# Splitting each of a weight's four loads into two transfers of rows

## The chip, the cores and the metric

The kernel runs on one core of a Trainium2 chip. The metric is the device time of one execution in microseconds (us). A measurement gives the median of several executions; three of the kernel before gave 159.38, 159.83 and 160.25 us.

## The reference

Two layers follow one another. The first is a linear attention with a decaying state: for each of 4 batches and 8 heads, 768 steps with heads 48 wide. The second mixes along the sequence through two low-rank matrices U and V (rank 32) and then along the channels through two weights, `w_ch1` (384 x 1536) and `w_ch2` (1536 x 384), with a ReLU between them.

```python
for t in range(S):
    state = alpha[:, :, t, :, None] * state + np.einsum('bhd,bhe->bhde', k[:, :, t], v[:, :, t])
    y[:, :, t] = np.einsum('bhd,bhde->bhe', q[:, :, t], state)
...
xt = x.transpose(0, 2, 1)
h = xt @ U @ V
u = x + h.transpose(0, 2, 1)
ch = np.maximum(u @ w_ch1, 0.0) @ w_ch2
return (u + ch).astype(np.float32)
```

## The kernel before

The sequence of 768 steps is cut into 6 chunks of 128. For each batch the kernel works through the chunks: it loads alpha, k, q and v of a chunk (four transfers of 192 KB), takes logarithms of alpha and sums them along the chunk with a matmul, scales k and q with the exponentials, and forms scores, state and output with matmuls. In some chunks two groups of heads are worked on as a pair. Then come the low-rank mix (`stage_mix`) and the two products with the weights: `mlp1` with `w_ch1` (L788 in the profile) and `mlp2` with `w_ch2` (L816).

Every piece of work is an operation of a plan (class `Plan`). Its order over all engines is a table of characters written out by hand or by a tool: three characters for each operation, which name it and the engine that does it. Each engine runs its own operations strictly in that order. A DMA is an operation too; nearly all are issued by SP (SyncE), in the table's order. Their completions are told by eight semaphores used in turn, so that an issue also waits until the transfer eight issues before it has landed.

The weights come from memory as float32 and are kept in SBUF as bfloat16. `weights` does this for both. `weights1` calls it for `w_ch1` with four groups of 384 columns (groups 0 to 3, operations `wload1 0` to `wload1 3`). One load (L323) brings a group as 128 partitions x 3 x 384 elements of 4 bytes, 576 KB, into the buffer `ws`, which lies in the memory of the second `h1t` tile (`h1t` in the profile). Three casts (L280 on ScalarE, L284 on GpSimd) then turn its three slices into bfloat16 in `w_sb`. The table issues the groups in the order 3, 1, 0, 2. `weights2` loads `w_ch2` in three transfers of 768 KB into the same buffer, once the casts have read it.

`mlp1` of the first batch needs a group for each three of its twelve slices `jt`: slice `jt` uses group `jt // 3`. In TensorE's order the first three products with the weight use group 3, and the fifth (with three matmuls each) is the first that uses group 1, the twelfth the first that uses group 0. Group 2 is used later, after other work.

Of the kernel before, what the change touches and what calls it, by code (L numbers as in the profile page):

```python
# [153 lines left out]
def kernel(  # L154
# [29 lines left out]
    def slots(name, n, shape, dtype):  # L184
        return [const.tile(shape, dtype, name=f"{name}{i}") for i in range(n)]

    PAIRS = {0: 3, 1: 3, 2: 0, 3: 0}
    QUEUE_T = tuple((3, c) for c in range(6))
    LAST, CUT = 3, 240
# [2 lines left out]
    P = Plan()  # L192
# [85 lines left out]
    def copy(eng, dst, src):  # L278
        if eng == "ACT":
            nc.scalar.copy(dst, src)  # L280
        elif eng == "DVE":
            nc.vector.tensor_copy(dst, src)  # L282
        else:
            nc.gpsimd.tensor_copy(dst, src)  # L284

    def queue(eng):
        return nc.scalar if eng == "ACT" else nc.sync
# [26 lines left out]
    ws = h1_s[1].bitcast(FP32)  # L314
# [5 lines left out]
    def weights(name, n, src, dst):  # L320
        for g in range(len(dst) // n):
            keys = [("ws", g * n + i) for i in range(n)]
            P.add(f"{name} {g}", lambda e, g=g: queue(e).dma_start(ws[:, g * n : (g + 1) * n, :], src(g)), w=keys)  # L323
            for i in range(n):
                to, key = dst[g * n + i]
                op = P.add("wcast", lambda e, to=to, x=g * n + i: copy(e, to, ws[:, x, :]), r=[keys[i]], w=[key])
                casts.setdefault(g * n + i, []).append(op)

    def weights1():
        cs = [slice(g * DM, (g + 1) * DM) for g in range(4)]  # L330
        weights(
            "wload1", NCT, lambda g: moe_w_ch1[:, cs[g]].rearrange("(c p) n -> p c n", p=128),
            [(w1_sb[:, ct, cs[g]], ("w1", g, ct)) for g in range(4) for ct in range(NCT)],
        )

    def weights2():
        weights(
            "wload2", 4, lambda g: moe_w_ch2[g * 512 : (g + 1) * 512, :].rearrange("(j p) n -> p j n", p=128),
            [(w2_sb[:, jt, :], ("w2", jt)) for jt in range(NJ)],
        )  # L340
# [3 lines left out]
    def paired(b, c):  # L344
        return c // 2 < PAIRS[b]

# [535 lines left out]
```

## Time and profile before

| what | us |
|---|---|
| median of three executions | 159.83 |
| lowest and highest | 159.38, 160.25 |
| the profiled execution's own time | 159.11 |
| its span in the profile | 157.3 |

The profile shows one execution. The span runs from the first to the last instruction of the program; the rest of the execution's time lies around it. PE is TensorE's matmul, PEld its weight load, DVE VectorE, ACT ScalarE, POOL GpSimd and SP SyncE. SPq stands for SP's queue of issues: the duration of such a row is how long SP was busy with an issue or held by it, not how long the data moved. The page's table of slices cuts the span in 40 equal parts; its row for TensorE reads

```profile
PE   6869899999989999999999999999999999999992
```

where each digit is the busy share in tenths (9 is 90% or more). Its DMA issues for the first weight (four transfers) and the second (three) are these, with the median time from issue to landing last:

```profile
h1t<-in_moe_w_ch_dram SPq DMA_DIRECT2D x4, 576.0 KB, 6.6
h1t<-in_moe_w_ch_dram SPq DMA_DIRECT2D x3, 768.0 KB, 8.7
```

### The profile page before, as it was taken

The numbers are of one execution on the slowest core, as the hardware profiler recorded it, in microseconds if no ns is written. First come the engines' busy times: TensorE is split into PE (matmuls) and PEld (weight loads), VectorE is DVE, ScalarE is ACT, GpSimd is POOL, SyncE is SP. The second block draws the span as 40 slices with busy tenths as digits, with TensorE's granted clock in tenths as the row PEclk, the third lists the DMA queues.
The fourth block names the chain that finished last, engine by engine and source line by source line (L and its number), as shares of the span: only waits on it lengthen the run. The fifth ranks groups of instructions, "written<-read, shape, count | busy, mean of one in ns | idle before, by whom it ended". The sixth has DMA issues, their size and how long they took to land.

```text
span 157.3 us, 4541 instructions
## 1 busy us (share of the span) xinstructions
PE 150.0 (95%) x1769; PEld 98.4 (63%) x1769; DVE 113.6 (72%) x252; ACT 85.0 (54%) x222; POOL 58.7 (37%) x94
## 2 busy tenths in 40 slices
PE   6869899999989999999999999999999999999992
PEld 2457676866767566766667656666657556665571
DVE  6349988996999348586999968698889247854151
ACT  3768887978867764749798484263612101061000
POOL 8188676465797110350726462048500000000000
PEclk9999999999999999999999999999999999999999
DMA  5999999997999799999999984899950556572425
GB/s 129 305 307 292 262 262 279 362 301 192 320 324 338 166 197 208 212 217 181 200 221 197 206 161 88 169 197 189 203 124 4 150 99 102 155 214 79 155 76 183
DMA packets 94230, 31.57 MB, mean 201 GB/s; under 512 B 87904, under 2 KB 94176, under 8 KB 94208
## 3 DMA queue, kind: packets, MB, share of 16 engines
q1 hardware_dynamic: 93680, 31.07, 81.9%
q8 instruction: 14, 0.23, 0.5%
q10 hardware_dynamic: 528, 0.20, 0.5%
q14 instruction: 8, 0.07, 0.1%
HBM read 23.79 MB, written 4.72 MB: 181 GB/s over the span
## 4 chain that ended last, share of the span: by engine, by line
PE 86%; SPq 3%; DMA 2%; POOL 2%; DVE 2%; issue 1%; ACT 1%; POOLq 0%; DVEq 0%; ACTq 0%
PE ps L816 30%; PE ps L788 29%; PE ps L431 3%; PE ps L737 3%; DMA io<-in_alpha_dram 2%; SPq L353 2%; PE ps L624 2%; PE ps L538 2%; PE ps L596 2%; PE ps L489 2%; POOL rkq L414 2%; PE ps L455 2%; PE ps L691 2%; PE ps L562 1%; PE ps L757 1%
## 5 line engine op out<-in xcount | busy, mean ns | idle before, releaser
L788 PE MATMUL ps<-uT,w_sb 128*128 128x384 bf16 x288 | 51.6, 326 | 0.5 <-DVE sm L518 0.5
L816 PE MATMUL ps<-w_sb,h1t 128*128 128x384 bf16 (+2 forms) x300 | 51.9, 320 | 0.0
L798 ACT ACTIVATE h1t<-ps 128x384 bf16<-128x384 f32 x49 | 23.1, 498 | 29.4 <-PE ps L788 29.4
L816 PEld LDWEIGHTS <-h1t 128*128 128x128 bf16 x300 | 27.5, 98 | 16.5 <-issue 0.6
L788 PEld LDWEIGHTS <-w_sb 128*128 128x128 bf16 x288 | 26.7, 98 | 16.6 <-issue 0.8
L800 DVE TENSOR_SCALAR h1t<-ps 128x384 bf16<-128x384 f32 x47 | 24.5, 550 | 5.3 <-PE ps L788 5.0
L822 DVE TENSOR_TENSOR io<-ub,ps 128x384 f32<-128x384 bf16 (+2 forms) x25 | 12.8, 533 | 13.9 <-PE ps L816 13.9
L738 DVE TENSOR_TENSOR ub<-xb,ps 128x384 bf16<-128x384 bf16 x24 | 12.1, 550 | 6.9 <-PE ps L737 6.6
L466 DVE TENSOR_TENSOR pm<-ps,maskp 128x512 bf16<-128x512 f32 x24 | 15.7, 681 | 0.5 <-PE ps L455 0.4
L634 DVE TENSOR_TENSOR pm<-ps,maskc 128x512 bf16<-128x512 f32 x24 | 15.3, 682 | 0.8 <-PE ps L624 0.8
L583 POOL TENSOR_TENSOR rkq<-io,aa 128x384 bf16<-128x384 f32 x8 | 7.3, 915 | 18.9 <-ACT aa L573 8.9
L583 POOL TENSOR_TENSOR rkq<-io,ai 128x384 bf16<-128x384 f32 x10 | 9.1, 914 | 10.1 <-PE ps L596 3.9
L414 POOL TENSOR_TENSOR rkq<-io,aa 128x384 bf16<-128x384 f32 x11 | 10.1, 923 | 7.2 <-DMA io<-in_q_dram 5.8
L280 ACT CAST xb<-ps 128x192 bf16<-128x192 f32 (+1 forms) x23 | 7.6, 360 | 8.5 <-PE ps L691 6.7
L280 ACT COPY kqt<-ps 128x512 bf16<-128x512 bf16 x15 | 8.9, 590 | 3.5 <-PE ps L431 1.8
L431 PE MATMUL ps<-ident,rkq 128*128 128x128 bf16 x96 | 8.4, 220 | 1.6 <-POOL rkq L414 1.6
L282 DVE COPY kqt<-ps 128x512 bf16<-128x512 bf16 x21 | 8.3, 416 | 2.3 <-PE ps L431 1.5
L414 POOL TENSOR_TENSOR rkq<-io,ai 128x384 bf16<-128x384 f32 x10 | 9.0, 912 | 1.1 <-PE ps L489 0.5
L573 ACT ACTIVATE aa<-ps 128x384 bf16<-128x384 f32 x12 | 6.0, 502 | 4.9 <-PE ps L564 4.1
L431 PEld LDWEIGHTS <-rkq 128*128 128x128 bf16 x96 | 6.0, 97 | 3.2 <-POOL rkq L414 2.3
L383 ACT ACTIVATE lt<-io 128x384 bf16<-128x384 f32 x12 | 6.2, 528 | 3.0 <-DMA io<-in_alpha_dram 2.9
L284 POOL CAST rv<-io 128x384 bf16<-128x384 f32 x14 | 7.0, 506 | 2.1 <-DMA io<-in_v_dram 1.6
(113 smaller groups left out, 220.8 us busy)
## 6 DMA issues: line engine op xcount, KB each, us to landing
io<-in_k_dram SPq DMA_DIRECT2D x24, 192.0 KB, 3.9
io<-in_q_dram SPq DMA_DIRECT2D x24, 192.0 KB, 3.9
io<-in_v_dram SPq DMA_DIRECT2D x24, 192.0 KB, 4.1
io<-in_alpha_dram SPq DMA_DIRECT2D x23, 192.0 KB, 4.0
h1t<-in_moe_w_ch_dram SPq DMA_DIRECT2D x4, 576.0 KB, 6.6
h1t<-in_moe_w_ch_dram SPq DMA_DIRECT2D x3, 768.0 KB, 8.7
out_dram<-io SPq DMA_DIRECT2D x24, 96.0 KB, 2.2
out_dram<-io SPq DMA_DIRECT2D x11, 192.0 KB, 1.9
```

Source lines behind the costliest of these rows:

```text
L280: nc.scalar.copy(dst, src)
L414: eng.tensor_tensor(jh(dst()[:, :, 0:D]), raw(a), jh(x()), op=ALU.mult)
L431: nc.tensor.matmul(dst, lhsT=ring()[:, HP * j + 2 * a : HP * j + 2 * a + 2, :].rearrange("t h w -> t (h w)"), rhs=ident, start=True, stop= ...
L466: nc.vector.tensor_tensor(dst, s2, maskp.to_broadcast([C, 2, 2, C]), op=ALU.mult)
L583: eng.tensor_tensor(dst()[:, :, 0:D], a(), x(), op=ALU.mult)
L634: nc.vector.tensor_tensor(pm()[:, :, par, :], s2, maskc.to_broadcast([C, HP, C]), op=ALU.mult)
L738: P.add(f"u {b}.{c}", lambda e, c=c, hb=hb: nc.vector.tensor_tensor(ub()[:, c, :], xb()[:, c, :], hb()[:, 0:DM], op=ALU.add), r=[hb] + xk( ...
L788: nc.tensor.matmul(hb()[:, 0:TW], lhsT=w1_sb[:, ct, jt * 128 : (jt + 1) * 128], rhs=u_half(uT, ct, tt, b in QUEUE_U), start=(ct == 0), sto ...
L798: nc.scalar.activation(dst, hb()[:, 0:TW], AF.Relu)
L800: nc.vector.tensor_scalar_max(dst, hb()[:, 0:TW], 0.0)
L816: nc.tensor.matmul(hb()[:, 0 : hi - lo], lhsT=h1()[:, jt, c * C : (c + 1) * C], rhs=w2_sb[:, jt, lo:hi], start=(jt == 0 and b not in INPLA ...
L822: P.add(f"out_{hi - lo} {b}.{c}", lambda e, hb=hb, lo=lo, hi=hi: nc.vector.tensor_tensor(flat(ou)[:, lo:hi], (xb if b in INPLACE else ub)( ...
```

## The change

A small table `ROWS` names, for each group of the first weight, how many of the 128 rows (partitions) the first transfer brings. A second transfer brings the rest. Both land in the same buffer and belong to the same operation of the plan, and the casts read the buffer after both. The second weight isn't in the table; its loads remain whole.

```diff
+    ROWS = {("wload1", 3): 120, ("wload1", 1): 104, ("wload1", 0): 120, ("wload1", 2): 88}
...
-            P.add(f"{name} {g}", lambda e, g=g: queue(e).dma_start(ws[:, g * n : (g + 1) * n, :], src(g)), w=keys)
+
+            def f(e, g=g):
+                cut = ROWS.get((name, g), 128)
+                for rows in (slice(0, cut), slice(cut, 128)):
+                    if rows.start < 128:
+                        queue(e).dma_start(ws[rows, g * n : (g + 1) * n, :], src(g)[rows])
+
+            P.add(f"{name} {g}", f, w=keys)
```

On SP, where the first three loads of the weight (groups 3, 1 and 0) are issued, the order before is this; `h1t_73` is the buffer of the weight, `io_...` are the buffers of k, q, v and alpha, and x2 stands for two such issues in a row.

```order
L353 DMA io_167<-in_q_dram 128x4x96
L323 DMA h1t_73<-in_moe_w_ch_dram 128x3x384 x2
L353 DMA io_168<-in_k_dram 128x4x96
L323 DMA h1t_73<-in_moe_w_ch_dram 128x3x384
L353 DMA io_169<-in_alpha_dram 128x4x96
L353 DMA io_170<-in_q_dram 128x4x96
```

With the change it is this; L331 is the line of the weight's loads now, and L363 that of the others.

```order
L363 DMA io_167<-in_q_dram 128x4x96
L331 DMA h1t_73<-in_moe_w_ch_dram 120x3x384
L331 DMA h1t_73<-in_moe_w_ch_dram 8x3x384
L331 DMA h1t_73<-in_moe_w_ch_dram 104x3x384
L331 DMA h1t_73<-in_moe_w_ch_dram 24x3x384
L363 DMA io_168<-in_k_dram 128x4x96
L331 DMA h1t_73<-in_moe_w_ch_dram 120x3x384
L331 DMA h1t_73<-in_moe_w_ch_dram 8x3x384
L363 DMA io_169<-in_alpha_dram 128x4x96
L363 DMA io_170<-in_q_dram 128x4x96
```

Three issues are added here; the loads of k, alpha and q keep their places among the rest and stand two, three and three issues further back.

Where the fourth load (group 2) is issued on SP, the order before is

```order
L353 DMA io_173<-in_v_dram 128x4x96
L353 DMA io_134<-in_k_dram 128x4x96
L323 DMA h1t_73<-in_moe_w_ch_dram 128x3x384
L353 DMA io_135<-in_v_dram 128x4x96
L353 DMA io_136<-in_k_dram 128x4x96
```

and with the change

```order
L363 DMA io_173<-in_v_dram 128x4x96
L363 DMA io_134<-in_k_dram 128x4x96
L331 DMA h1t_73<-in_moe_w_ch_dram 88x3x384
L331 DMA h1t_73<-in_moe_w_ch_dram 40x3x384
L363 DMA io_135<-in_v_dram 128x4x96
L363 DMA io_136<-in_k_dram 128x4x96
```

The loads of v and k behind it stand four issues further back. Nothing moves on the other engines: their instructions and their order are the same.

## The prediction

> **What bounds the kernel now.** I read the page's table of engines first, then stages cut where the change begins, then TensorE's own waits.
>
> ```profile
> PE 150.0 (95%) x1769; PEld 98.4 (63%) x1769; DVE 113.6 (72%) x252; ACT 85.0 (54%) x222; POOL 58.7 (37%) x94
> 0.00:24.00 24.00, 20.16 (x352) 13.66 (x353) 16.44 (x54) 17.06 (x44) 16.44 (x34) 1.00 0.98 259
> 24.00:44.00 20.00, 20.00 (x302) 13.84 (x302) 18.16 (x42) 16.66 (x43) 12.05 (x20) 1.00 1.01 292
> 44.00:50.00 6.00, 5.47 (x149) 4.16 (x142) 5.70 (x13) 4.48 (x15) 4.94 (x9) 1.00 1.03 329
> 50.00:155.00 105.00, 104.36 (x986) 66.79 (x983) 73.35 (x145) 46.84 (x122) 25.25 (x35) 1.00 0.76 165
> ```
>
> The stage rows give, after the stretch and its length, the busy time of PE, PEld, DVE, ACT and POOL, the granted clock (1.00 everywhere), the DMA share and GB/s. Up to 24 us TensorE loses 24.00 - 20.16 = 3.84 us; the DMA share there is 0.98, so this first stage waits for data. From 24 to 155 us it is busy 20.00 + 5.47 + 104.36 = 129.83 of 131.00 us. Behind 24 us the kernel is bound by TensorE with 1.17 us lost: 0.53 between 44 and 50 us and 0.64 after that.
>
> ```profile
> 23.88 1.62 SPq L323 DMA_DIRECT2D h1t<-in_moe_w_ch_dram  x2
> 25.54 1.48 SPq L353 DMA_DIRECT2D io<-in_k_dram  x1
> 27.07 0.74 SPq L323 DMA_DIRECT2D h1t<-in_moe_w_ch_dram  x1
> 27.86 0.49 SPq L353 DMA_DIRECT2D io<-in_alpha_dram  x1
> 28.39 1.43 SPq L353 DMA_DIRECT2D io<-in_q_dram  x1
> 29.86 1.75 SPq L353 DMA_DIRECT2D io<-in_v_dram  x1
> 31.66 0.68 SPq L353 DMA_DIRECT2D io<-in_q_dram  x1
> 32.38 1.45 SPq L353 DMA_DIRECT2D io<-in_v_dram  x1
> 33.94 1.84 SPq L353 DMA_DIRECT2D io<-in_k_dram  x1
> 35.83 0.66 SPq L323 DMA_DIRECT2D h1t<-in_moe_w_ch_dram  x1
> 36.58 0.43 SPq L353 DMA_DIRECT2D io<-in_v_dram  x1
> ```
>
> These are SP's rows of the timeline (start, duration, what). The four loads of the first weight are issued at 23.88 (parts 3 and 1, one behind the other), 27.07 (part 0) and 35.83 (part 2). So nothing before 23.88 us can change, and what the change can win is at most the 1.17 us that TensorE loses behind it: 0.7% of this execution's 159.11 us (span 157.3 and 1.81 around it). What it can cost has no such lid.
>
> **The change part by part.** *More issues.* Four transfers are added on SP. A plain issue takes 0.43 to 0.68 us there (27.86, 31.66, 36.58), take 0.51, so 2.04 us of SP's time. Three of them come before 33.94 us, where five issues last 1.48, 1.43, 1.75, 1.45 and 1.84 us. Against 0.51 each that is 7.95 - 2.55 = 5.40 us in which SP was held, and I read this as transfers queued faster than they drain. Three more issues, 1.53 us, are taken out of that 5.40 and cost nothing. If the queue had room there, they would push the four loads behind them by 1.53 us. The fourth stands behind 35.83 and is not covered: v at 36.58 and the three loads behind it go 0.51 us later. Their readers:
>
> ```profile
> 37.04 1.78 POOL L414 TENSOR_TENSOR rkq<-io,aa 128x384 bf16<-128x384 f32 x2 [2.04 <-DMA io<-in_q_dram]
> 39.04 0.91 POOL L414 TENSOR_TENSOR rkq<-io,ai 128x384 bf16<-128x384 f32 x1 [0.22 <-PE ps L788]
> 42.94 1.78 POOL L414 TENSOR_TENSOR rkq<-io,ai 128x384 bf16<-128x384 f32 x2
> 44.68 2.04 POOL L414 TENSOR_TENSOR rkq<-io,aa 128x384 bf16<-128x384 f32 x2
> io<-in_k_dram SPq DMA_DIRECT2D x2, 192.0 KB, 4.9
> ```
>
> At 4.9 us to landing, the k issued at 37.11 to 38.27 is there at 42.0 to 43.2 us; the two products at 42.94 each take 0.89, so the second begins at 43.83: 0.6 us to spare against 0.51. I take zero.
>
> *The data.* The bytes are the same, 576 KB a load. What is not in the trace is how the rows of a transfer of 120, 104 or 88 rows are laid over the 16 DMA engines, since every load before has 128 (v_in 32). I bound the landing from two sides.
>
> ```profile
> 28.00:30.00 2.00, 2.00 (x38) 1.65 (x36) 2.00 (x5) 1.94 (x8) 1.20 (x2) 1.00 1.05 364
> 35.40:36.40 1.00, 1.00 (x9) 0.59 (x6) 1.00 (x3) 1.00 (x4) 0.00 (x0) 1.00 0.24 58
> GB/s 330 437 227 146 146 192 165 158 165 211 284 303 277 238 173 108 65 54 50 46 19 19 23 19 84 169 157 119 146 219 296 315 277 242 181 161 123 223 96 65
> ```
>
> While weights flow, 364 GB/s: one load takes 589,824 B / 364 = 1.62 us, and one engine of 16 carries 364 / 16 = 22.8 GB/s. *Upper end:* each small part runs behind its big one as long as its rows ask for, on engines that are already full: 1.62 us x 8/120, 24/104, 8/120, 40/88 = 0.11, 0.37, 0.11, 0.74. *Lower end,* below nothing: in the last row (40 slices of 0.1 us from 34 us on) the rate falls to 19 GB/s from 36.0 to 36.4 us, less than one engine's. So one engine was still at work long after the rest: from 35.4 to 36.4 us the moved rate is 58 GB/s, and the issue at 33.94 is held until 35.78. If the split spares this late engine its rows, each load could land earlier by up to the second that the tail shows, 1.0 us. Between -1.0 and the sums (0.11, 0.48, 0.59 for the three that follow one another; 0.74 for part 2, in front of which the queue ran empty), I take zero: the same engines and rate as the nearest row, the 128-row load.
>
> *What a landing is worth to TensorE.* The casts and the first product of the weight:
>
> ```profile
> 30.29 0.50 POOL L284 CAST w_sb<-h1t 128x384 bf16<-128x384 f32 x1 [1.02 <-DMA h1t<-in_moe_w_ch_dram]
> 30.49 0.97 ACT L280 CAST w_sb<-h1t 128x384 bf16<-128x384 f32 x2
> 31.85 0.96 POOL L284 CAST w_sb<-h1t 128x384 bf16<-128x384 f32 x2 [1.06 <-DMA h1t<-in_moe_w_ch_dram]
> 34.04 0.96 POOL L284 CAST w_sb<-h1t 128x384 bf16<-128x384 f32 x2 [0.76 <-DMA h1t<-in_moe_w_ch_dram]
> 40.89 0.93 ACT L280 CAST w_sb<-h1t 128x384 bf16<-128x384 f32 x2 [0.27 <-DMA h1t<-in_moe_w_ch_dram]
> 31.69 6.01 PE L788 MATMUL ps<-uT,w_sb 128*128 128x384 bf16 x36
> 42.39 1.14 PE L788 MATMUL ps<-uT,w_sb 128*128 128x384 bf16 x6
> ```
>
> The idle time in brackets says that these casts begin as the load lands: 30.29, 31.85, 34.04, 40.89. Part 3: ScalarE's casts end at 31.46, TensorE starts at 31.69, and 0.20 us lie between landing and the casts' start, so 0.43 us are free. Part 1 is wanted by the fifth of the twelve groups of three: 31.69 + 12 x 0.162 = 33.63 (36 matmuls until 37.53), POOL is done at 32.81: 0.82 free. Part 0 is wanted by the twelfth, 31.69 + 33 x 0.162 = 37.04, done at 35.00 on POOL: 2.0 free. Part 2 is wanted at 42.39, ScalarE is done at 41.82: 0.57 free. The upper end uses 0.11 of 0.43, 0.48 of 0.82, 0.59 of 2.0, and 0.74 of 0.57: only part 2 reaches TensorE, by 0.17 us. An earlier landing wins nothing at these four places, because TensorE has no gap there (20.00 of 20.00 us): it is late for its own earlier work, not for the weight.
>
> *The 0.53 us.*
>
> ```profile
> 46.25 0.65 PE L788 MATMUL ps<-uT,w_sb 128*128 128x384 bf16 x3 [0.53 <-DVE sm L518]
> ```
>
> This wait ends with a VectorE sum, not with a load. It can go or stay with the way that POOL's work falls beside VectorE's; bounds -0.53 and 0, I take half, -0.26.
>
> **Sum:** 159.11 + 0 (issues) + 0 (landings) - 0.26 = 158.85 for the profiled execution. That execution lies 0.72 below the median of the runs shown, 159.83; carried to the median: **159.6 us**.
>
> [...] The trace does not show which engines carry which rows. [...]
>
> **The rivals.** *A, faster: the late engine is spared.* For it: the 19 GB/s tail, the 1.84 us issue behind it, and POOL's 2.04 us of waiting for q at 37.04. The loads behind part 0 would land up to 1.0 us earlier and SP would go on earlier. Against it: TensorE has only 1.17 us to give back, of which no part ends with a load. If all 0.53 goes, and the runs' 0.72 over the profile is also time lost to late loads, 159.83 - 1.25 = **158.6**.
>
> *B, slower: the late engine gets more.* The mechanism is the landing of part 2. If its rows fall on engines that carry the big part too, and the late engine is one of them, the four extra lots add up, 0.11 + 0.37 + 0.11 + 0.74 = 1.33 us, against 0.57 free: TensorE waits 0.76 us at 42.39 us. The casts of part 2 must also be over before the second weight's loads overwrite the buffer:
>
> ```profile
> 42.04 1.04 SPq L323 DMA_DIRECT2D h1t<-in_moe_w_ch_dram  x2
> 49.24 0.95 ACT L280 CAST w_sb<-h1t 128x384 bf16<-128x384 f32 x2
> 50.63 0.82 PE L816 MATMUL ps<-w_sb,h1t 128*128 128x384 bf16 x4
> ```
>
> There the second weight is cast until 50.19 and wanted at 50.63, so 0.44 is free for the first of them; the one behind it goes out later by the same 0.76. I price a second wait of equal size for it: 159.83 + 1.52 = **161.3**. The point from which B decides: part 2 landing more than 0.57 us later. For it: of the three later loads the one landing at 40.89 has the least room, and its small part, 40 rows, is the largest. Against it: the queue had run empty in front of it (0.24 share), so lags need not add up.
>
> *C: it does not do what it says.* The rows stay spread evenly over all engines, whatever their number; then four issues are all that remains, and the time is that of the forecast without the half of 0.53: 159.8.
>
> **How the numbers follow.** Forecast 0.36, C 0.12, A 0.28, B 0.24. The likeliest time is 159.6, and its own range 159.1 to 160.5. The range over the cases reaches to A's 158.6, and to B's 161.3: **158.6 to 161.3**; what lies outside is A with more than 1.25 us or B with a third wait. A measurement of this kernel can tell about 0.5% from no change, 0.8 us. A's 158.6 is 0.77% below the median, B's 0.9% above it, so the chances are 0.28 faster, 0.48 the same, 0.24 slower.
>
> **What the changed profile would show.** Forecast right: TensorE again loses about 1.2 us between 24 and 155 us, and its first product of the weight starts within 0.1 us of 31.69. A: SP's held issues shrink (1.84 at 33.94 first), POOL's 2.04 us wait for q goes, the tail of 19 GB/s near 36 us is gone, and casts begin before 30.29, 31.85 and 34.04. B: ScalarE's casts of part 2 begin after 41.5 us and TensorE shows a gap before the product that stood at 42.39, and another near 50 to 53 us. The issue term is wrong if the loads behind 36.58 land more than 0.6 us later and POOL waits for k at 43.8. The forecast as a whole is wrong if time changes before 23.88 us, where nothing was touched.

## The result, and the profile after

The changed kernel takes 165.72 us (median of three executions, 165.42 to 166.05) against 159.83 us (159.38 to 160.25). The ratio is 1.037 with a 95% interval of 1.0315 to 1.0425: slower by 5.89 us, far outside the range of the prediction. The profiled execution took 166.05 us, its span is 164.3 us, 7.0 more than before. The times and ratios of the experiments below leave out executions that took over 1.5% longer than the fastest of the same kernel (two of four of e4, one of four of e5, two of ten of e1, e9 and e12, one of ten of e11), and the profiles of e1, e4 and e9 show such executions.

From the page of the kernel after: busy time of each engine, granted clock in 40 slices, DMA packets, and the costliest group.

```profile
PE 152.4 (93%) x1768; PEld 99.1 (60%) x1769; DVE 114.0 (69%) x252; ACT 84.9 (52%) x222; POOL 59.1 (36%) x94
PEclk9999999999986999999999999999999999999999
DMA packets 94258, 31.57 MB, mean 192 GB/s; under 512 B 87932, under 2 KB 94204, under 8 KB 94236
L798 PE MATMUL ps<-uT,w_sb 128*128 128x384 bf16 x288 | 53.6, 330 | 4.4 <-POOL w_sb L287 4.0
```

L798 is the product that was L788, L331 the weight's loads, L283 and L287 the casts on ScalarE and GpSimd. The last row is new in kind: TensorE stood idle for 4.4 us ahead of this product, 4.0 of it for weights that GpSimd had not cast yet. The same stretches as in the prediction, after the change:

```profile
0.00:24.00 24.00, 19.83 (x351) 13.68 (x353) 16.31 (x54) 16.87 (x44) 15.61 (x33) 1.00 0.99 258
24.00:44.00 20.00, 17.43 (x228) 11.00 (x230) 15.25 (x34) 14.21 (x36) 9.80 (x15) 1.00 1.00 224
44.00:50.00 6.00, 4.02 (x48) 2.37 (x47) 3.45 (x9) 2.24 (x7) 3.50 (x7) 0.86 0.99 207
50.00:155.00 105.00, 104.92 (x1101) 67.72 (x1100) 76.24 (x151) 51.56 (x136) 30.23 (x42) 0.99 0.84 177
48.00:50.00 2.00, 1.93 (x7) 0.85 (x8) 0.56 (x1) 1.57 (x5) 2.00 (x4) 0.59 0.76 190
50.00:52.00 2.00, 2.00 (x60) 1.66 (x59) 0.92 (x3) 0.81 (x2) 2.00 (x3) 0.56 0.90 249
```

Between 24 and 50 us TensorE loses 2.57 + 1.98 = 4.55 us, before 0.53: 4.02 more. Behind 50 us it loses nothing that matters (0.08). Its busy time is 2.4 us longer, and the two short rows show where much of that is: from 48 to 52 us the granted clock was 0.59 and 0.56, and 3.93 us busy at some 0.575 of the clock are the work of 2.26, so about 1.7 us by this estimate. The stretch up to 24 us, which the change does not touch, lost 4.17 instead of 3.84. So 4.02 + 2.4 + 0.33 make 6.75 of the 7.0 us.

Read the DMA columns of the second and third row: the share stays at 1.00 and 0.99, yet the rate is 224 and 207 GB/s instead of 292 and 329. **The DMA engines were as busy as before and moved 23% and 37% less.** Where TensorE waited (timeline of the kernel after, TensorE; in brackets the idle time and what ended it):

```profile
32.26 2.33 PE L798 MATMUL ps<-uT,w_sb 128*128 128x384 bf16 x12 [0.42 <-POOL w_sb L287]
35.93 4.25 PE L798 MATMUL ps<-uT,w_sb 128*128 128x384 bf16 x22 [1.34 <-POOL w_sb L287]
40.67 0.50 PE L798 MATMUL ps<-uT,w_sb 128*128 128x384 bf16 x2 [0.49 <-POOL w_sb L287]
48.03 2.16 PE L798 MATMUL ps<-uT,w_sb 128*128 128x384 bf16 x6 [1.79 <-POOL w_sb L287]
```

These four waits are 4.04 us, as much as the extra loss. And the casts that they wait for, from GpSimd's timeline and ScalarE's:

```profile
31.70 0.50 POOL L287 CAST w_sb<-h1t 128x384 bf16<-128x384 f32 x1 [1.56 <-DMA h1t<-in_moe_w_ch_dram]
35.37 0.96 POOL L287 CAST w_sb<-h1t 128x384 bf16<-128x384 f32 x2 [3.17 <-DMA h1t<-in_moe_w_ch_dram]
39.66 0.96 POOL L287 CAST w_sb<-h1t 128x384 bf16<-128x384 f32 x2 [2.56 <-DMA h1t<-in_moe_w_ch_dram]
47.43 0.93 ACT L283 CAST w_sb<-h1t 128x384 bf16<-128x384 f32 x2 [3.33 <-DMA h1t<-in_moe_w_ch_dram]
```

Each cast itself waited for its load. Against the casts at 30.29, 31.85, 34.04 and 40.89 us before, the four groups come 1.4, 3.5, 5.6 and 6.5 us later; the prediction had found 0.43, 0.82, 2.0 and 0.57 us of room. The delay grows from load to load; that each stands behind the one before it in the queue is the likely reason.

### The profile page after: what moved, and what is told of

Same layout as the page of the kernel before. It is cut to its first block, busy times and chain, and to the rows that moved or that the text cites. A ratio compares the mean times of both kernels' runs of the same rounds, so it can differ in the third digit from the quotient of the medians.

```text
span 164.3 us, 4551 instructions
## 1 busy us (share of the span) xinstructions
PE 152.4 (93%) x1768; PEld 99.1 (60%) x1769; DVE 114.0 (69%) x252; ACT 84.9 (52%) x222; POOL 59.1 (36%) x94
## 2 busy tenths in 40 slices
DMA packets 94258, 31.57 MB, mean 192 GB/s; under 512 B 87932, under 2 KB 94204, under 8 KB 94236
## 4 chain that ended last, share of the span: by engine, by line
PE 68%; SPq 19%; DMA 9%; issue 2%; DVE 0%; POOL 0%; DVEq 0%; POOLq 0%
PE ps L826 29%; PE ps L798 24%; SPq L363 18%; DMA h1t<-in_moe_w_ch_dram 9%; PE ps L634 2%; PE ps L747 2%; PE ps L606 2%; PE ps L701 1%; PE ps L572 1%; PE ps L696 1%; PE ps L548 1%; PE ps L657 1%; PE ps L716 1%; PE ps L465 1%; PE ps L767 1%
## 5 line engine op out<-in xcount | busy, mean ns | idle before, releaser
L798 PE MATMUL ps<-uT,w_sb 128*128 128x384 bf16 x288 | 53.6, 330 | 4.4 <-POOL w_sb L287 4.0
L798 PEld LDWEIGHTS <-w_sb 128*128 128x128 bf16 x288 | 26.7, 98 | 22.2 <-POOL w_sb L287 5.3
L283 ACT CAST xb<-ps 128x192 bf16<-128x192 f32 (+1 forms) x23 | 7.6, 362 | 9.2 <-PE ps L701 6.7
L283 ACT COPY kqt<-ps 128x512 bf16<-128x512 bf16 x15 | 8.9, 591 | 3.1 <-PE ps L441 1.6
L283 ACT CAST w_sb<-h1t 128x384 bf16<-128x384 f32 x14 | 6.5, 520 | 6.7 <-DMA h1t<-in_moe_w_ch_dram 6.7
L287 POOL CAST w_sb<-h1t 128x384 bf16<-128x384 f32 x10 | 4.8, 507 | 11.0 <-DMA h1t<-in_moe_w_ch_dram 11.0
```

What stands on the lines that cost most here:

```text
L798: nc.tensor.matmul(hb()[:, 0:TW], lhsT=w1_sb[:, ct, jt * 128 : (jt + 1) * 128], rhs=u_half(uT, ct, tt, b in QUEUE_U), start=(ct == 0), sto ...
```

## The experiments

Fifteen kernels were run. Each group has the kernel before run beside it on the same chip; ratios are against that. The common gauge is the row from 28 to 32 us, where the weight's loads flow among those of q, alpha and v. Before and after, from the view by stretches (last columns: clock, DMA share, GB/s) and the DMA view of the same stretch (packets, MB, share of 16 engines). Before:

```profile
28.00:32.00 4.00, 4.00 (x88) 3.26 (x87) 4.00 (x11) 3.94 (x12) 1.85 (x4) 1.00 1.06 362
...
q1 hardware_dynamic: 1439, 1.44, 105.8%
```

After:

```profile
28.00:32.00 4.00, 3.76 (x86) 3.00 (x83) 3.98 (x11) 2.96 (x9) 1.73 (x3) 1.00 1.01 224
...
q1 hardware_dynamic: 763, 0.89, 100.6%
```

In 4 us, 16 engines have 64 engine-microseconds. Before, 1.44 MB in 1.058 x 64 is 21.3 GB/s for each busy engine; after, 0.89 MB in 1.006 x 64 is 13.8. The engines do not stand idle, they are slow: 0.65 of their rate. (The share adds up the times of the packets and can pass 1.00 a little.)

### Is it the issues, or the cut by rows?

Four theories stood at the start: the four extra issues (with the eight semaphores they use), unequal shares of rows on the engines, a late engine, and the rate of the engines.

e1 keeps the number of issues but cuts within the rows: each transfer has all 128 rows, the first brings two of a row's three slices of 384 elements, the second the third:

```diff
-                for rows in (slice(0, cut), slice(cut, 128)):
+                for part in ((slice(0, 2), slice(2, 3)) if name == "wload1" else (slice(0, n),)):
...
+                    queue(e).dma_start(ws[:, g * n + part.start : g * n + part.stop, :], src(g)[:, part, :])
```

> Each of the four loads is issued as two transfers again, but cut along the free side: 128x2x384 and 128x1x384, so SP has the same four more issues and every transfer keeps its 128 rows. Theory 'slow rows' (a transfer of other than 128 rows moves slower on all engines at once; the changed kernel moved 214 GB/s between 28 and 30 us at a DMA share of 0.97, before 364 at 1.05): 159.8 us, within 0.8, and 320 GB/s or more from 28 to 32 us. Theory 'late engine' (some engines get more rows, and one of them is the late one): 159.8, within 0.8. Theory 'issues' (four more issues and completions on SP): 165 to 166 us.

Measured: 159.39 us, ratio 1.000 (0.9966 to 1.0034).

```profile
28.00:32.00 4.00, 4.00 (x65) 2.74 (x63) 3.40 (x9) 3.68 (x11) 2.05 (x4) 0.98 1.02 340
```

The same issues cost nothing, and the rate stays at 340 GB/s. What costs is that the rows are cut. e2 cuts all four loads in halves, e4 all four at 120:

```diff
-    ROWS = {("wload1", 3): 120, ("wload1", 1): 104, ("wload1", 0): 120, ("wload1", 2): 88}
+    ROWS = {("wload1", 3): 64, ("wload1", 1): 64, ("wload1", 0): 64, ("wload1", 2): 64}
```

```diff
-    ROWS = {("wload1", 3): 120, ("wload1", 1): 104, ("wload1", 0): 120, ("wload1", 2): 88}
+    ROWS = {("wload1", 3): 120, ("wload1", 1): 120, ("wload1", 0): 120, ("wload1", 2): 120}
```

> All four loads cut into 64 and 64 rows, two equal halves, as many issues as in the change. 'Slow rows': the rate falls as in the changed kernel or further, below 260 GB/s from 28 to 32 us, and 163 to 168 us. 'Late engine': 64 rows divide evenly over 16 engines, each has 8 rows in all as before: 159.8, within 0.8, and 320 GB/s or more. 'Issues': 165 to 166.

> All four loads cut into 120 and 8 rows. 'Slow rows': the 120 rows of each load move slowly, so most of the 5.9 us stay: 163 to 166 us. 'Late engine': at most one row in eight more per engine and load, four times 1.62/8 = 0.8 us by the last load, of which little reaches TensorE: 159.8 to 160.6. 'Issues': 165 to 166.

Measured: e2 163.2 us (162.44 to 163.66), ratio 1.0241 (1.0204 to 1.0279); e4 162.26 us (two executions, 161.67 and 162.85), ratio 1.0187 (1.0129 to 1.0245). Their rows, e2 first:

```profile
28.00:32.00 4.00, 2.82 (x43) 2.02 (x42) 3.33 (x8) 3.30 (x9) 1.42 (x2) 1.00 1.07 228
...
q1 hardware_dynamic: 771, 0.91, 107.0%
```

```profile
28.00:32.00 4.00, 3.96 (x60) 3.08 (x58) 3.85 (x9) 3.94 (x12) 1.42 (x2) 1.00 1.02 224
```

The theory of slow rows fits both, though e4 lies 0.7 us under its range. Halves are as slow as the change's cuts, at 0.91 MB in 1.070 x 64, 13.3 GB/s for each busy engine. A late engine that gets too many rows is not likely to be the main cause, since 64 rows divide evenly by 16, and the 94294 packets on e2's page say, by the count further below, that all 16 engines took part in each transfer.

e5 cuts the fourth load alone, at 88, and e8 the first three alone, as the change does:

```diff
-    ROWS = {("wload1", 3): 120, ("wload1", 1): 104, ("wload1", 0): 120, ("wload1", 2): 88}
+    ROWS = {("wload1", 2): 88}
```

```diff
-    ROWS = {("wload1", 3): 120, ("wload1", 1): 104, ("wload1", 0): 120, ("wload1", 2): 88}
+    ROWS = {("wload1", 3): 120, ("wload1", 1): 104, ("wload1", 0): 120}
```

> Only the load that is issued last (group 2) is cut, into 88 and 40 rows; the other three are whole. 'Slow rows': this load takes about twice its 1.6 us and lands 1.5 to 3 us later; TensorE waits 1 to 2.4 us for it: 160.8 to 163. 'Late engine': up to half of 1.62 us later, 0.8, less 0.57 that is free: 159.8 to 160.8. 'Issues': a quarter of the 5.9 us: 161.3.

> The changed kernel with the load that is issued last (group 2) whole again: only the first three are cut, 120, 104 and 120 rows. If the cost of the loads adds up, this has what is left of 5.9 us when the 2.6 us of that load alone are taken off: 162.0 to 163.2. If the delays hide one another (a later load that waits behind earlier ones costs little more): 163.5 to 165. If the last load were the cause of all: 159.3 to 160.1.

Measured: e5 161.75 us (161.18 to 162.66), ratio 1.0166 (1.0096 to 1.0235); e8 162.12 us (162.03 to 164.28), ratio 1.021 (1.0103 to 1.0318). Both parts of the change cost. Against their own runs of the kernel before (159.30 and 159.16) they are 2.45 and 2.96 us slower. The sum, 5.41, is near the whole 5.89, but the intervals are too wide to say that the parts simply add up. In e5 the fourth group's casts begin late, as they should (ScalarE's timeline):

```profile
43.21 0.92 ACT L283 CAST w_sb<-h1t 128x384 bf16<-128x384 f32 x2 [1.84 <-DMA h1t<-in_moe_w_ch_dram]
```

That is 2.3 us behind the 40.89 of before, although this load was issued earlier, at 34.55 us instead of 35.83. But in this profiled run TensorE loses only 0.6 us more between 24 and 50 us; another 0.9 was lost before 24 us, and 0.9 behind its last product. So how e5's 2.45 us come about is not settled.

### Is it the reading side?

In `w_ch1` neighbouring rows lie 6,144 bytes apart. e6 keeps the change's cuts and reads from `w_ch2`, where they lie 1,536 bytes apart; e7 has the whole loads of before (the line that the change removes) from that source. With either kernel the first product has other values for its weight; sizes and types are the same. Both carry this edit:

```diff
-            "wload1", NCT, lambda g: moe_w_ch1[:, cs[g]].rearrange("(c p) n -> p c n", p=128),
+            "wload1", NCT, lambda g: moe_w_ch2[g * DM : (g + 1) * DM, :].rearrange("(c p) n -> p c n", p=128),
```

> The changed kernel with its four cuts, but the first weight's loads read from the second weight's array, where the 128 rows of a slice lie 1,536 bytes apart, end to end, and not 6,144; the first product then has other values for its weight, sizes and types are the same. Theory 'write side' (the slowness comes from where the rows are written on the chip): no change against the changed kernel, 164.5 to 166.5 us and 200 to 240 GB/s from 28 to 32 us. Theory 'read side' (it comes from the order in which rows are read from memory): the rate returns to 320 GB/s or more and the time to 159.3 to 160.5.

> The kernel before, whole loads, with the same source as the run beside it (the first weight read from the second weight's array, so its values are others). Both theories: 159.3, within 0.8; it is the zero point of that run. If it is itself faster or slower by over 0.5%, the spacing of rows matters by itself.

Measured: e6 165.19 us, ratio 1.0353 (1.029 to 1.0416); e7 159.97 us, ratio 1.0026 (0.9992 to 1.006). The place of the rows in memory makes no difference that these runs can tell: the cuts cost the same from this source. e6's row:

```profile
28.00:32.00 4.00, 4.00 (x64) 3.25 (x61) 3.85 (x11) 3.71 (x11) 1.42 (x2) 1.00 0.91 238
```

### How many engines, and how evenly?

The packets tell how many engines a transfer runs on. Suppose that each engine of a transfer leaves one small completion packet: then the four whole loads leave 64. The change has 28 packets more on its page (94258 against 94230), all of them of 4 bytes in the trace, so 92. That is the sum of 15 + 8, 13 + 12, 15 + 8 and 11 + 10, the largest divisors of the rows that are not above 16; the pages show the sums alone. The same count gives 28 more for e4, 5 for e5 and 20 for e13 below, and their pages have 94258, 94235 and 94250. e3 cuts at 112 and 16, e14 at 80 and 48, both multiples of 16; e13 cuts all four at 88 and 40.

```diff
-    ROWS = {("wload1", 3): 120, ("wload1", 1): 104, ("wload1", 0): 120, ("wload1", 2): 88}
+    ROWS = {("wload1", 3): 112, ("wload1", 1): 112, ("wload1", 0): 112, ("wload1", 2): 112}
```

```diff
-    ROWS = {("wload1", 3): 120, ("wload1", 1): 104, ("wload1", 0): 120, ("wload1", 2): 88}
+    ROWS = {("wload1", 3): 80, ("wload1", 1): 80, ("wload1", 0): 80, ("wload1", 2): 80}
```

```diff
-    ROWS = {("wload1", 3): 120, ("wload1", 1): 104, ("wload1", 0): 120, ("wload1", 2): 88}
+    ROWS = {("wload1", 3): 88, ("wload1", 1): 88, ("wload1", 0): 88, ("wload1", 2): 88}
```

> All four loads cut into 112 and 16 rows. Both numbers divide by 16, so that each of 16 engines can carry 7 rows and 1, eight in all as before. 'Slow rows, whatever the count' (only a transfer of all 128 rows is fast): 220 to 260 GB/s from 28 to 32 us and 162 to 164 us, as with 64 and 64 rows (163.2) and 120 and 8 (163.6). 'Too few engines' (120, 104 and 88 rows are slow because they do not divide by 16, and 64 rows for another reason): 320 GB/s or more, 159.3 to 160.1.

> All four loads cut into 88 and 40 rows, neither a multiple of 16. By the rows of the change (92 completions for its eight transfers, as the number of packets shows, where 16 each would make 128) such a cut runs on 11 and on 10 engines, of which ten then carry 8 + 4 = 12 rows. Theory 'slow writing alone': as the even cuts, 162 to 163.6 us. Theory 'slow writing and unequal shares': the ten engines have half as much again to do, 165 to 169 us.

> All four loads cut into 80 and 48 rows, both multiples of 16: every engine has 5 + 3 = 8 rows, with transfers of nearly the sizes of the run beside it. Both theories: as the even cuts, 162 to 163.6 us; the distance to the run beside it is the price of the unequal shares, nothing by 'slow writing alone', 2 us or more by the other.

Measured: e3 162.4 us (160.88 to 162.48), ratio 1.016 (1.0083 to 1.0237); e13 166.11 us (165.08 to 167.37), ratio 1.0416 (1.0336 to 1.0495); e14 163.18 us (162.61 to 163.91), ratio 1.024 (1.0186 to 1.0294). The rows of e3, e13 and e14, in this order:

```profile
28.00:32.00 4.00, 3.81 (x77) 3.14 (x79) 3.98 (x10) 2.97 (x9) 1.42 (x2) 1.00 1.10 242
```

```profile
28.00:32.00 4.00, 3.58 (x55) 2.81 (x54) 3.67 (x9) 3.32 (x9) 1.41 (x2) 1.00 0.85 212
```

```profile
28.00:32.00 4.00, 3.92 (x60) 3.10 (x59) 3.85 (x10) 3.84 (x11) 1.60 (x3) 1.00 0.99 216
```

The page of e3 and that of e14 have 94294 packets, 64 more than before: by this count all 16 engines took part in each transfer. Equal numbers of rows for each are an estimate, from 16 dividing every one of these cuts. Still they are slow. So the low rate does not seem to need unequal shares. But these seem to add to it: e13 and e14 differ by 2.93 us, and of the three only e13's DMA share falls, to 0.85, as it would where engines stand idle while others have rows left. Which engines carry rows of both parts no run shows. The prediction's term for the landings had been about this part alone.

### How must rows be cut to be slow?

e9, e10 and e11 cut only the fourth load, into 2, 4 and 8 blocks of neighbouring rows; e12 cuts it into 9 pieces of 128 rows x 128 columns.

```diff
...
+                step = 32 if (name, g) == ("wload1", 2) else 128
+                for at in range(0, 128, step):
+                    queue(e).dma_start(ws[at : at + step, g * n : (g + 1) * n, :], src(g)[at : at + step])
```

That is e10; e9 and e11 have 64 and 16 in place of 32. And e12:

```diff
...
+                if (name, g) == ("wload1", 2):
+                    for c in range(3):
+                        for at in range(0, DM, 128):
+                            queue(e).dma_start(ws[:, g * n + c, at : at + 128], src(g)[:, c, at : at + 128])
```

> Only the load that is issued last (group 2) is cut, into 2 transfers of 64 rows. All four runs of this set cut that load alone, to ask what the write side counts. Theory 'places' (neighbouring rows share a place of writing; a transfer of few neighbouring rows reaches few places, 64 rows half of them): the load moves at half the rate, as in the run of all four at 64 and 64, 215 to 240 GB/s while it moves, 160.8 to 162.5 us. Theory 'more, smaller transfers': slower with each further cut, here least of the three, 160 to 161.5.

> The same load in 4 transfers of 32 rows. [...] 'More, smaller transfers': more than the run of 64s by 0.8 us or more.

> The same load in 8 transfers of 16 rows. [...] 'More, smaller transfers': eight issues of 0.4 us, 3.2 us for the load, which goes out as fast as it is issued: 161 to 163.5, and the run with nine pieces of all rows costs as much.

> The same load in 9 transfers of all 128 rows, 128 elements (512 bytes) of each: more issues than any other run of this set, no row cut. 'Places': only the nine issues count, 9 x 0.4 = 3.6 us of SP's time, two to three us later landing at most and less than with 16s: 159.3 to 162. 'More, smaller transfers': as slow as the run of 16s or slower.

Measured: 160.22, 160.68, 161.24 and 160.80 us, ratios 1.0032 (0.9986 to 1.0078), 1.0059 (1.0021 to 1.0096), 1.0071 (1.0027 to 1.0115) and 1.0067 (1.003 to 1.0104). The theory of places missed in e9, whose time lies below its range; the theory of more, smaller transfers missed in e10, which took 0.46 us more than e9 and not 0.8. By halves alone the fourth load did become slower: its packets of 1,536 bytes took a median of 87 ns in e9 and 65 before. That cost the kernel nothing that can be told. Eight blocks of 16 rows and nine pieces of 128 rows cost the same, but both are paced by SP: their issues take 3.78 us for 8 and 4.31 us for 9, about 0.47 us each, so 576 KB could not come faster than that whatever the engines do. What blocks of 32 or 16 rows would do to a full queue is thus not shown.

The question is better asked with two transfers for each load, which e15 does. It has e2's numbers, 64 and 64 rows in all four loads, but one transfer brings the even rows and one the odd ones:

```diff
...
+                for rows in ((slice(0, 128, 2), slice(1, 128, 2)) if name == "wload1" else (slice(0, 128),)):
+                    queue(e).dma_start(ws[rows, g * n : (g + 1) * n, :], src(g)[rows])
```

> All four loads cut into the 64 even and the 64 odd rows, in place of the lower and the upper half. Theory 'halves reach half of the places of writing' alone: every second row reaches all places, so 320 GB/s or more from 28 to 32 us and 159.3 to 160.5 us. Theory 'any transfer of other than 128 neighbouring rows has its engines writing to shared places': 215 to 260 GB/s and 162 to 164 us, as with halves.

Measured: 160.04 us (158.96 to 160.58), ratio 1.0044 (1.0012 to 1.0076).

```profile
28.00:32.00 4.00, 4.00 (x64) 3.21 (x62) 3.85 (x11) 3.93 (x13) 1.92 (x3) 1.00 0.93 303
...
q1 hardware_dynamic: 1206, 1.20, 92.4%
```

Here 1.20 MB in 0.924 x 64 is 20.3 GB/s for each busy engine, nearly the 21.3 of before. The number of rows, the bytes, the issues and the number of packets (94294) are those of e2; the ratio is 1.0044 instead of 1.0241, which leaves a small loss, as its interval does not reach 1. The time is what the theory of places expected, the rate a little less than its 320 GB/s.

The single packets in the traces say the same. The first 1,152 packets of 1,536 bytes are the first three loads. Their median time was 65 ns before, and again 65 in e1 and in e15; it was 106 in the change, 113 in e2, 105 in e3 and 112 in e4 and in e14. So it is not another mix of transfers that lowers the rate of the stretch; packets of the same size take longer. **From e2 to e15 only which rows go together has changed: cutting a load into two blocks of neighbouring rows is what makes the engines slow.**

Why neighbouring rows are slow is not shown. That they share places of writing was the author's theory; no run shows where on the chip a row is written, nor which engine writes it. The theory fits 228 GB/s for e2, in a stretch that holds other loads too, and 303 for e15, whose halves are interleaved. It does not by itself cover e3 and e4, whose big parts of 112 and 120 rows are nearly the whole load and about as slow (242 and 224 GB/s).

## Why the prediction was wrong

**The step that failed** is the one on the data. It bounded the landings by "1.62 us x 8/120, 24/104, 8/120, 40/88 = 0.11, 0.37, 0.11, 0.74" and took zero, "the same engines and rate as the nearest row, the 128-row load". Even its upper end lets the big part run at the 364 GB/s of a whole load. The runs put 13.8 in place of 21.3 GB/s for each busy engine. So the four landings were late by 1.4, 3.5, 5.6 and 6.5 us, where the upper ends were 0.11, 0.48, 0.59 and 0.74. In the stretch from 28 to 32 us 224 GB/s moved in place of 362, and on that the result turned: e15, with the same issues and the rate nearly kept, lost 0.4%.

**The issues** were priced right: nothing. e1 has the same four and a ratio of 1.000. The reason given was weaker than the price. The prediction read SP's held issues as a queue that drains too slowly, but the view of what SP waited for before, from 33 to 37 us, puts the longest of them, the one at 33.94 us, down to ScalarE:

```profile
SPq L353 <- ACT tot L408: 1.8, 1, 1.8
```

That four more issues are hidden is also shown only where the rate holds; after the change SP itself ran late, and issued group 2 at 39.48 us instead of 35.83 (SP's queue in the timeline of after):

```profile
39.48 0.97 SPq L331 DMA_DIRECT2D h1t<-in_moe_w_ch_dram  x2
```

This is how the delay of the first three loads is handed to the fourth.

**The room** at the four places was right, and with it TensorE waits 4 us more and not 6.5: the third group had 2.0 us, and a wait for one group is also time in which the next one comes nearer. The 0.53 us of which half was taken off decide nothing: in the profile of the kernel after this wait is gone, and in e6, with the same cuts, it is 0.51. The lid on gains, 1.17 us, was too high as well: its 0.64 behind 50 us were not lost to anything. TensorE's last product of before ends at 153.83 + 0.54 = 154.37 us (its timeline), and the stretch was cut at 155.

```profile
153.83 0.54 PE L816 MATMUL ps<-w_sb,h1t 128*128 128x144 bf16 x6
```

**Rival A**, a late engine that is spared, did not come: no kernel with cut rows was faster. **Rival C**, rows spread evenly whatever their number, is refuted by the packets, if the count above holds: 92 completions where 16 engines for each of eight transfers would leave 128. **Rival B** had the sign, and the place in part: part 2 did land late and TensorE waited for it, but 1.79 us instead of 0.76, and three earlier groups, which B had let pass, added 2.25 us. B's second wait did not come: the second weight's first product starts without idle time, although the room there was smaller than the 0.44 us of the prediction, which left out GpSimd's casts of the same load (until 50.47 us, against 50.63). B's mechanism, more rows on the engines that carry the big part, is supported by e13 and e14, where it would be worth about 2.9 us. It is the smaller part: e14 and e2, which have none of it if the shares are equal, still lose 2.4%.

**The granted clock** fell to 0.59 and 0.56 behind the wait of 1.79 us, a cost that no term of the prediction held. In e13 it fell to five tenths (the slice from 49.4 to 53.6 us of its page) behind a wait of 2.1 us at the same place; in e6, where this wait was 1.6 us, it was 1.00 from 48 to 52 us. It is not needed for the result: e6 took 165.19 us without it, and another execution of the kernel after, whose mean granted clock was 0.999 instead of 0.99, took 165.72 us. Where that one lost the time instead, no profile shows.

**Open** are which engine carries which rows and where they are written, with it why neighbouring rows are slow, and e5's 2.45 us. The 0.33 us before 24 us are no more than executions differ by there: no cut touches that stretch, and TensorE lost 4.28 us in it in the profile of e15 and 4.77 in that of e5. No version beat the kernel before; whole loads of 128 rows, or cuts within the rows as in e1, are the best that was measured.

## What to carry to other kernels

When a transfer's rows are cut, price the rate and not only the balance: look at MB over busy engine time in the stretch, since a DMA share of 1.00 says nothing about how fast the busy engines are (21.3 GB/s each at 1.06, 13.8 at 1.01). If a load has to be split, split it within the rows (e1, ratio 1.000), or interleave its rows (e15, 1.0044), and prefer numbers of rows that 16 divides (e14 took 2.93 us less than e13); two blocks of neighbouring rows cost a third or more of the rate here (212 to 242 GB/s in place of 362). Where loads queue behind one another, room at one place is not enough: add the delays up along the queue before comparing them with it (here they grew from 1.4 to 6.5 us over four loads).

## What the hardware showed that was not expected

- Two blocks of neighbouring rows bring a busy DMA engine, on average, from 21.3 down to 13.3 to 13.8 GB/s in the change, e2, e3, e4 and e14 (15.6 in e13, 16.4 in e6), even where by the count of packets all 16 engines were at work (e2, 13.3); even and odd rows of the same number give 20.3 (e15). A packet of 1,536 bytes takes a median of 113 ns in e2 and 65 in e15.
- A block of 8 rows cut from 128 (e4) slows the stretch as much as halves do: 224 and 228 GB/s.
- After a wait of 1.79 us TensorE was granted 0.59 and 0.56 of its clock for some 4 us in the profiled execution; in e13, after 2.1 us, it was five tenths of it, and in e6, after 1.6, the whole.
